# First batch of a fused linear-attention and ResMLP kernel: k^T v kept raw and times g in one operand, W_tok and W_ch1 loaded in pieces by GpSimd's queue, and the instruction order read from a table

## The chip, the core and the metric

The kernel runs on one core of one Trainium2 chip. The metric is the device time of one execution in microseconds (us). TensorE (PE) does the matmuls, VectorE (DVE), ScalarE (ACT) and GpSimd (POOL) the rest; SyncE (SP) and GpSimd issue the DMAs, each in the order of its own queue.

## The reference, cut to what matters

```python
# q, k, v: [8 batches, 8 heads, 576, 64];  x: [8, 576, 512]
kv  = einsum('bhsd,bhse->bhde', k, v)
out = einsum('bhsd,bhde->bhse', q, kv)
rms = sqrt(mean(out * out, axis=-1, keepdims=True) + 1e-06)
x   = (out / rms * g_norm)            # heads side by side: [8, 576, 512]
a1  = alpha1 * x + beta1
u   = x + lam * einsum('ts,bsd->btd', w_tok, a1)       # token mixing, 576 x 576
a2  = alpha2 * u + beta2
y   = u + lam * (maximum(a2 @ w_ch1, 0) @ w_ch2)       # 512 -> 2048 -> 512
```

## The kernel before, in words

Everything is recorded as operations (class Op) with their reads and writes, and then put in order. Batch after batch the stages are: kv (k^T v for pairs of heads, two heads to a matmul, only the diagonal blocks kept, in `kvc`), norm (q times kv, squares, sums, square root, reciprocal, and the scaling to x and to r, the operand of the token mixing), tok (token mixing with the transposed W_tok in `wt`, then the addition to x), a2 (alpha2, beta2 and the transposition of u), ch1 (64 matmuls of 512 columns against W_ch1, ReLU on ScalarE) and ch2 (64 matmuls against W_ch2; finish multiplies by lam, adds and stores). A main tile of 512 tokens goes by batch; the last 64 tokens of two batches go together (the tail: ch1_tail, and column group c = 4 of ch2).

**Batch 0 is done in halves** (j = 0, 1: four heads each), so that the first channel matmuls can begin early. load_half (L616) brings q, k and v in pairs of heads of 288 KB through SP's queue. qt_early (L693) interleaves two pairs of q (L698, GpSimd) and transposes them on PE in fp32 (L703). kv_first (L719) multiplies k by v (L725) and copies the result to `kvc` (L736 DVE, L739 ACT). norm_half (L854) makes q.kv in matmuls of 128 columns (L864), and norm_ops (L793) follows: Square (L807 ACT), sum (L810 DVE), Sqrt (L813 ACT), reciprocal (L816 DVE), x (L828 DVE), r = x times e1 (L831, GpSimd or DVE), x times g (L833, GpSimd). e1 is the row alpha1 x lam x 8 g, spread over the partitions by a matmul (L678). wt_group (L1077) transposes W_tok, loaded in fp32 by one DMA on SP's queue (L629) and one for the last 64 rows (L631), by fp32 transposes on PE (L1081, L1084), and ACT copies them (L1087). wsums (L1097) makes column sums of it (L1103, L1105) for the beta1 term; these go to rows of `wt` (L1110 ACT, L1113 DVE), and every token mixing reads them with its fifth slice. tok_half (L924) is the token mixing of a half (L929, addition L937 on DVE), a2_pair (L965) the transposition of u (L968 PE, L972 ACT).

Batch 1 has its q pairs loaded and transposed as in batch 0 (L703, L713), its k and v by GpSimd's queue (L1186, L1190); kv(1) is L749 and L755, norm(1) L843. From batch 1 on, a2_dma (L976) makes a2 by two GpSimd passes (L986, L989) and a transposing DMA (L993). W_ch1 and W_ch2 are cast to bf16 by their DMAs, which only GpSimd's queue issues (L1163, L1169); W_ch1 comes as one quarter, one quarter and one half.

**The order.** `schedule` (L135) plans the program when it is built: due times, a list of hand-set shifts (L1283) and gates (L1298, extra dependencies), and costs in us decide which operation each engine takes next. PE takes "main" matmuls (ch1, ch2) in their order and fits "fill" matmuls (all others) between or weaves a float32r or fp32 one with a bf16 one. Until the first main matmul, idle time of PE and the gaps of fp32 matmuls are filled with matmuls of 128 columns on a constant tile `fil` (L597, here called fillers; `fil` is set by the memset L596). Every engine then executes its own list in order; an instruction that waits holds up all behind it on its engine.

Of the kernel before, what the change touches and what calls it, by code (L numbers as in the profile page):

```python
# [7 lines left out]
F32 = mybir.dt.float32  # L8
# [7 lines left out]
NH = 8  # L16
# [7 lines left out]

class Op:


    __slots__ = ("bias", "q", "kind", "cost", "lat", "fns", "pri", "idx", "deps", "raw", "alloc",
                 "tiles", "start", "end", "pos", "waits", "inc", "clock", "slot", "nbytes",
                 "val", "margin", "tag", "narrow", "urgent", "ns")  # L30

    def __init__(self, q, kind, cost, lat, fns, pri, idx):
        self.q, self.kind, self.cost, self.lat = q, kind, cost, lat
        self.fns, self.pri, self.idx = fns, pri, idx
        self.deps, self.raw = set(), set()
        self.alloc, self.tiles = [], []
        self.start = self.end = self.pos = None
        self.waits, self.inc, self.clock = [], False, None
        self.slot = self.nbytes = self.val = self.ns = None
        self.margin = 0.0  # L40
        self.tag, self.narrow, self.urgent = "", False, False
# [12 lines left out]
class Prog:  # L54
    ENGINES = ("PE", "ACT", "DVE", "POOL")

    def __init__(self, nc, stack):
# [7 lines left out]
        self.main, self.fill = [], []  # L65
        self.bias = 0.0
        self.reach = 24
        self.warm, self.began, self.early, self.lead = 6.0, False, 45.0, 100.0
        self.t0, self.pace, self.last, self.shift = 31.0, 1.28, None, {}
        self.gate = {}  # L70
# [4 lines left out]
    def _add(self, o, r, w, after):  # L75
# [10 lines left out]
        for key in w:  # L86
# [5 lines left out]
            for y in self.readers.get(key, ()):  # L92
                if y is not o:
                    o.deps.add(y)
                    if not isinstance(key, Bank) and key[0] == "sm":
                        o.raw.add(y)
# [11 lines left out]
    def op(self, q, cost, fn, r=(), w=(), pri=0.0, lat=0.15, after=()):  # L108
        o = Op(q, "c", cost, lat, [fn], self.bias + pri, len(self.ops))
        o.bias = self.bias  # L110
        return self._add(o, r, w, after)

    def dma(self, q, slot, nbytes, fn, r=(), w=(), pri=0.0, after=(), issue=0.55):
        o = Op(q, "d", issue, 0.0, [fn], self.bias + pri, len(self.ops))
        o.slot = slot
        o.nbytes, o.ns = nbytes if isinstance(nbytes, tuple) else (nbytes, 20.0)
        o.bias = self.bias
        return self._add(o, r, w, after)

    def mm(self, stream, cols, fns, r=(), w=(), slow=False, after=(), margin=0.3,  # L120
           urgent=False):

        n = len(fns)
        per = cols * MM_NS + 0.0025
        each = slow if isinstance(slow, float) else {"r": 0.213}.get(slow, 0.109)
        o = Op("PE", "w" if slow and each is not slow else "m",
               n * (max(per, each) if slow else max(per, 0.056)),
               0.24, fns, self.bias, len(self.ops))
        o.bias = self.bias
        o.margin, o.narrow, o.urgent = 0.0 if urgent else margin, cols < 512, urgent  # L130
        (self.main if stream == "main" else self.fill).append(o)
        return self._add(o, r, w, after)


    def schedule(self):  # L135
        for i, j in self.gate.items():
            self.ops[i].deps.add(self.ops[j])
        due, t = {}, self.t0
        for o in self.main:
            due[o] = t  # L140
            t += o.cost * self.pace
        after = {}
        for o in self.ops:
            for y in o.deps:
                after.setdefault(y, []).append(o)
        order, left = [], {o: len(after.get(o, ())) for o in self.ops}
        stack = [o for o in self.ops if not left[o]]
        while stack:
            o = stack.pop()
            order.append(o)  # L150
            for y in o.deps:
                left[y] -= 1
                if not left[y]:
                    stack.append(y)
        for o in order:
            d = due.get(o, 1e6)
            for y in after.get(o, ()):
                if y in due:
                    d = min(d, due[y] - o.cost - o.lat - (2.5 if o.kind == "d" else 0.0))
            if d < 1e6:  # L160
                due[o] = d
        for o in self.ops:
            if o.kind == "d":
                o.pri += self.shift.get(o.idx, 0.0)
            elif o in due and o.pri - o.bias > -900:
                o.pri = due[o] + self.shift.get(o.idx, 0.0)
            elif o.pri - o.bias > -900:
                o.pri = 1e4 + o.pri
        self.fill.sort(key=lambda o: o.pri)
        queues = {e: [] for e in ("ACT", "DVE", "POOL", "SP")}  # L170
        for o in self.ops:
            if o.q != "PE":
                queues[o.q].append(o)
        for q in queues.values():
            q.sort(key=lambda o: (o.pri, o.idx))
        main, fill = list(self.main), list(self.fill)
        self.main0 = set(self.main)
        free = {e: 0.7 for e in list(queues) + ["PE"]}
        owner = [None] * 8
        rings = {e: deque() for e in ("SP", "POOL", "ACT")}  # L180
        t, left = 0.0, len(self.ops)
        events = {0.7}
        self.sequence = []
        self.idle = []
        last_fill = False
        INF = 1e9

        def ready_at(o):
            m = 0.0
            for y in o.deps:  # L190
                if y.end is None:
                    return INF
                m = max(m, y.end - y.lat if y.q == o.q == "PE" else y.end)
            return m

        def bank_at(b):
# [1137 lines left out]
```

## Time and profile before

| what | us |
|---|---|
| three runs | 356.01, 356.05, 357.27 |
| median of the runs | 356.05 |
| profiled execution, first to last instruction (its span) | 354.8 |
| so outside the span, against the median | 1.25 |
| PE busy in the span | 341.3 |
| DVE, POOL, ACT busy | 189.8, 161.4, 149.0 |

Busy time of PE counts a matmul from its start to its modelled end, and matmuls overlap; so the rate is read from start to start, and a busy PE may be doing fillers. "Chain" below is the profile's chain of work that ended last, followed back from the last instruction: start, duration, what. In the table of stretches each engine has its busy time and, in brackets, its instructions, then the granted clock of PE, the share of the DMA engines and GB/s.

### The profile page before, as it was taken

The page shows a single profiled execution, that of the slowest core. Times are in us where ns is not written, and L with a number is a line of the kernel's source. Part 1 is how long each engine was busy: PE and PEld are TensorE (multiplying, and loading weights), DVE is VectorE, ACT ScalarE, POOL GpSimd, SP SyncE. Part 2 cuts the span into 40 slices and gives each one's busy share as a digit, 9 for nine tenths or more (in the row PEclk, how much of TensorE's full clock was granted, in tenths as well). Part 3 has the DMA queues.
Part 4 walks back from the last instruction along what each step waited for, and adds up shares of the span by engine and source line. Part 5 has one row for each costly group of instructions (what it writes and reads, how often), then busy time and mean ns, then how long its engine had stood idle before and what let it go on. Part 6 is the DMA issues. An engine that isn't in the chain of part 4 may idle for free.

```text
span 354.8 us, 5512 instructions
## 1 busy us (share of the span) xinstructions
PE 341.3 (96%) x2208; PEld 198.4 (56%) x2241; DVE 189.8 (54%) x343; ACT 149.0 (42%) x291; POOL 161.4 (45%) x151
## 2 busy tenths in 40 slices
PE   4979999999999999999999999999999999999994
PEld 3858964454664664466556545564476444444644
DVE  3475778204685579636745676459444963210043
ACT  3335397004940386126823366136552273026400
POOL 2397410965308940985058612973192306930000
PEclk9989999999999999999999999999999999999999
DMA  7999899969598399138963995239922110330012
GB/s 241 267 336 161 139 251 230 144 110 198 120 262 134 90 232 213 31 93 195 247 61 76 221 173 124 46 116 258 175 33 89 59 31 15 75 105 0 2 69 79
DMA packets 107952, 48.76 MB, mean 137 GB/s; under 512 B 81997, under 2 KB 99925, under 8 KB 107928
## 3 DMA queue, kind: packets, MB, share of 16 engines
q1 hardware_dynamic: 82312, 27.71, 42.9%
q0 software_dynamic: 25616, 20.71, 34.0%
q8 instruction: 17, 0.28, 0.3%
q14 instruction: 7, 0.06, 0.1%
HBM read 38.82 MB, written 9.44 MB: 136 GB/s over the span
## 4 chain that ended last, share of the span: by engine, by line
PE 87%; DMA 5%; SPq 2%; POOL 2%; DVE 1%; issue 1%; ACT 0%; DVEq 0%; POOLq 0%
PE ps L1031 31%; PE ps L1002 31%; PE ps L914 8%; PE ps L1014 4%; PE ps L843 3%; DMA hh<-in_moe_w_tok_dram 2%; PE ps L749 2%; DMA w<-in_k_dram 2%; PE ps L597 1%; SPq L611 1%; PE ps L929 1%; POOL a1f L986 1%; PE ps L948 1%; PE ps L1081 1%; PE ps L1042 1%; DMA lam_bc<-in_moe_lam_dram 1%
## 5 line engine op out<-in xcount | busy, mean ns | idle before, releaser
L1031 PE MATMUL ps<-w,hh 128*128 128x512 bf16 x543 | 135.3, 383 | 0.7 <-issue 0.3
L1002 PE MATMUL ps<-a2m,w 128*128 128x512 bf16 x501 | 117.8, 381 | 1.0 <-DVE tmp L1058 0.4
L997 ACT ACTIVATE hh<-ps 128x512 bf16<-128x512 f32 x144 | 84.8, 597 | 64.3 <-PE ps L1002 54.9
L1031 PEld LDWEIGHTS ps<-w,hh 128*128 128x128 bf16 x560 | 52.9, 97 | 58.8 <-issue 1.6
L1002 PEld LDWEIGHTS ps<-a2m,w 128*128 128x128 bf16 x512 | 48.7, 98 | 56.5 <-DVE tmp L1058 1.3
L986 POOL TENSOR_TENSOR a1f<-xm,a_bc 128x512 f32<-128x512 f32 x28 | 35.5, 1273 | 68.6 <-DVE xm L921 68.3
L1058 DVE TENSOR_TENSOR tmp<-ps,lam_bc 128x512 f32<-128x512 f32 (+2 forms) x38 | 25.1, 661 | 69.8 <-PE ps L1031 56.5
L1063 POOL TENSOR_TENSOR xm<-xm,tmp 128x512 f32<-128x512 f32 x28 | 35.4, 1269 | 34.7 <-DVE tmp L1058 34.7
L810 DVE TENSOR_REDUCE small<-sq 128x8 f32<-128x512 f32 (+2 forms) x41 | 27.2, 666 | 25.2 <-ACT sq L807 25.0
L989 POOL TENSOR_TENSOR a2b<-a1f,b_bc 128x512 bf16<-128x512 f32 x32 | 40.3, 1273 | 0.7
L843 PE MATMUL ps<-kvc,qt 128*128 128x128 f32 x140 | 40.1, 395 | 0.0
L921 DVE TENSOR_TENSOR xm<-ps,xm 128x512 f32<-128x512 f32 x28 | 19.3, 690 | 29.8 <-PE ps L914 28.5
L749 PE MATMUL ps<-vr,kr 128*128 128x128 f32 x112 | 32.3, 395 | 0.0
L807 ACT ACTIVATE sq<-ps 128x512 f32<-128x512 f32 (+2 forms) x41 | 23.9, 584 | 19.3 <-PE ps L843 18.5
L1199 ACT ACTIVATE qt<-qp 128x576 fp32r<-128x576 f32 x24 | 15.9, 682 | 32.3 <-DVE qp L1196 32.3
L843 PEld LDWEIGHTS ps<-kvc,qt 128*128 128x128 f32 x140 | 27.4, 199 | 2.0
L914 PE MATMUL ps<-rm,wt 128*128 128x512 bf16 x109 | 28.3, 379 | 0.2
L597 PE MATMUL ps<-fil 128*128 128x128 bf16 x109 | 20.0, 245 | 4.5 <-DVE fil L596 4.5
L819 DVE TENSOR_TENSOR ps<-ps,small 128x512 f32<-128x512 f32 (+1 forms) x35 | 23.5, 690 | 0.5
L766 ACT ACTIVATE kvo<-ps 64x256 f32<-64x256 f32 x14 | 5.3, 378 | 43.0 <-PE ps L755 42.8
L749 PEld LDWEIGHTS ps<-vr,kr 128*128 128x128 f32 x112 | 22.3, 201 | 0.9
L1196 DVE STREAM_TRANSPOSE qp<-qs 128x576 f32<-128x576 f32 x24 | 17.3, 755 | 5.6 <-DMA qs<-in_q_dram 3.4
(109 smaller groups left out, 324.0 us busy)
## 6 DMA issues: line engine op xcount, KB each, us to landing
out_dram<-xm SPq DMA_DIRECT2D x32, 256.0 KB, 2.3
kr<-in_k_dram POOLq DMA_DIRECT2D x7, 1024.0 KB, 9.0
vr<-in_v_dram POOLq DMA_DIRECT2D x7, 1024.0 KB, 11.4
qs<-in_q_dram SPq DMA_DIRECT2D x24, 288.0 KB, 11.1
w<-in_moe_w_ch_dram POOLq DMA_DIRECT2D x3, 1024.0 KB, 10.2
xm<-in_q_dram SPq DMA_DIRECT2D x8, 288.0 KB, 4.4
w<-in_k_dram SPq DMA_DIRECT2D x4, 288.0 KB, 5.6
qs<-in_v_dram SPq DMA_DIRECT2D x4, 288.0 KB, 5.9
```

Source lines behind the costliest of these rows:

```text
L749: P.mm("fill", 128, [lambda e, t=t, c=c, h=h, o=128 * (h % 4): e.matmul(t.ap()[:, o:o + 128], kr4[:, h, c:c + 2, :].rearrange("p c d -> p ...
L807: P.op("ACT", act(n), lambda e: e.activation(sq[rs, s3, 0:nst, :].rearrange("p h e -> p (h e)"), ps(), ACT.Square), r=[t], w=[("sq", s3)])
L810: P.op("DVE", dve(n), lambda e: e.tensor_reduce(out=st, in_=sq[rs, s3, 0:nst, :], axis=AX.X, op=ALU.add), r=[("sq", s3)], w=[("sm", s4)])
L843: P.mm("fill", 128, [lambda e, p=p: e.matmul(dst(p), qt[:, p, cs], kvc[:, i, p, :], start=(p == 0), stop=(p == 3)) for p in range(4)], r=[ ...
L914: P.mm("fill", 512, [lambda e, sc=sc: e.matmul(t.ap(), wt[:, sc if sc < 4 else tw(b), 128 * c:128 * c + 128], rsrc(b, sc, al), start=(sc = ...
L986: P.op("POOL", pool(512), lambda e: e.tensor_tensor(out=a1f[:, s], in0=x, in1=a2_bc[:], op=ALU.mult), r=ks + ["a2"], w=[("a1f", s)])
L989: P.op("POOL", pool(512), lambda e: e.tensor_tensor(out=a2b[:, c], in0=a1f[:, s], in1=b2_bc[:], op=ALU.add), r=[("a1f", s), "b2"], w=[("a2 ...
L997: P.op("ACT", act(512), lambda e: e.activation(dst, t.ap(), ACT.Relu), r=[t], w=keys, pri=-1000)
L1002: P.mm("main", 512, [lambda e, dj=dj: e.matmul(t.ap(), w1[:, dj, 128 * fj:128 * fj + 128], a2m[:, b % 3, dj, :], start=(dj == 0), stop=(dj ...
L1031: P.mm("main", 512, [lambda e, fj=fj, t=t, c=c: e.matmul(t.ap(), (ht[:, fj, 128 * c:128 * c + 128] if c < 4 else hl[:, fj, :]), w2[:, fj, ...
L1058: P.op("DVE", dve(z - a), lambda e: e.tensor_tensor(out=tmp[:, s, a:z], in0=t.ap()[:, 0:z - a], in1=lam_bc[:, a:z], op=ALU.mult), r=[t, "l ...
L1063: lambda e: e.tensor_tensor(out=x, in0=x, in1=tmp[:, s, a:z], op=ALU.add),
```

## The change

The scheduler is gone; `replay` takes the order of all 1439 operations with their PSUM banks from a table (ORDER), with fillers written as ~n and woven matmuls as a+b, and a new list of gates (GATES). Besides:

- kv_first writes k^T v twice: raw (ACT, `kvc` slot 0) and times 8g (DVE, slot 1). norm_half multiplies q by both in one float32r matmul of 256 columns; the squares are taken from the raw half, x = (q.kv.g) times the reciprocal, and r = x times `la` (alpha1 x lam) is one GpSimd pass. The GpSimd pass x times g of batch 0 is gone. g comes by a broadcast DMA; e1 for the later batches is la x g, one GpSimd pass.
- W_tok is cast to bf16 by three DMAs on GpSimd's queue (behind a gate: the last copy of the first half's k^T v). Its transposes are bf16 matmuls against a bf16 identity, `idb`; the copies alternate between ACT and DVE.
- tok_half is cut in two matmul groups, the slices 0 to 3 and the slice 4, so that only the second waits for the column sums. a2_pair alternates ACT and DVE.
- W_ch1 and W_ch2 come in quarters. In batch 1, r of the four main column groups is a GpSimd pass, the addition of tok goes to PSUM and a1f is made from there by DVE, with a copy to x by ACT.
- In the odd batches ch2 takes column group 4 before 3, so that the last tile, which is cut in three, is a main one of 128 rows with one store each.

```diff
-        P.schedule()
+        P.replay(ORDER, GATES)
...
+ORDER = """
+33 3 7 4 30 14 0 27 ~35 13 6 5 32 12 28 15 204 10 1 29 9 2 31 203 35 8 17 11 34 41 42 16 59:1 18
...
+GATES = {12: 4, 16: 15, 18: 6, 22: 58, 26: 203, 37: 35, 38: 21, 39: 44, 40: 1, 122: 142, 184: 74,
...
+    def replay(self, order, gates):
+        for i, j in gates.items():
             self.ops[i].deps.add(self.ops[j])
+        for word in order.split():
+            if word[0] == "~":
+                self.sequence.append((self.idler(int(word[1:])),))
+                continue
+            unit = []
+            for part in word.split("+"):
...
+                at, *banks = part.split(":")
+                o = self.ops[int(at)]
...
+        for c in (0, 2):
+            P.dma("POOL", "wl%d" % c, dcost(256, 105), lambda e, c=c: e.dma_start(
+                wl[:, c:c + 2, :], moe_w_tok[128 * c:128 * c + 256, :].rearrange(
+                    "(c p) s -> p c s", p=128)), w=[("wl", c), ("wl", c + 1)], issue=0.9)
+        P.dma("POOL", "wlt", dcost(64, 190), lambda e: e.dma_start(
+            wlt, moe_w_tok[512:576, :]), w=["wlt"], issue=0.8)
...
+                    raw, dst = (kvc[rs, i, 2 * j + s, 64 * m:64 * m + 64] for i in range(2))
+                    P.op("ACT", act(64), lambda e, raw=raw, src=src: e.activation(
+                        raw, src(), ACT.Identity), r=[t], w=[("kv%d" % m, 0, 2 * j + s)])
+                    P.op("DVE", dve(64), lambda e, dst=dst, src=src, rs=rs: e.tensor_tensor(
+                        out=dst, in0=src(), in1=g_bc[rs, :], op=ALU.mult), r=[t, "g"],
...
             P.mm("fill", 128, [lambda e, c=c, cs=cs, s=s: e.matmul(
-                dst(c, s), qt[:, 2 * j + s, cs], kvc[:, 0, 2 * j + s, :],
+                dst(c, s), qt[:, 2 * j + s, cs], kvc[:, :, 2 * j + s, :],
...
+            P.op("POOL", pool(w), lambda e: e.tensor_tensor(
+                out=r, in0=x, in1=la_bc[rs, None, fs].to_broadcast([rs.stop - rs.start, n, 256]),
...
-            for c in range(2 * ch, 2 * ch + 2):
+            for scs in (range(4), (4,)):
...
-        load_w1(0, 1, q2)
-        load_w1(1, 1, q3, 1)
+        load_w1(0, 1)
         for p in range(4):
-            load_pair(1, "q", q, q1s, p, k3)
-        load_w1(2, 2, v3, 2)
+            load_pair(1, "q", q, q1s, p)
+        for i in range(1, 4):
+            load_w1(i, 1)
...
-            cs = range(5 if b % 2 else 4)
+            cs = (0, 1, 2, 4, 3) if b % 2 else (0, 1, 2, 3)
```

Read out in words, the table gives these orders up to the second batch's channel matmuls. **PE:** 35 fillers; the spreading of la; 9 transposes of q (half 0); k^T v of half 0 with 5 and 10 fillers behind its two pairs; 9 transposes of q (half 1); q.kv of column groups 4, 2 and 3 of half 0; k^T v of half 1; q.kv of groups 0 and 1 of half 0; 14 fillers; q.kv of groups 2 and 3 of half 1; the 25 W_tok transposes, with 9, 5, 7 and 3 fillers and the rest of q.kv of half 1 among them; column sums and token mixing of half 0 (slices 0 to 3, then 4); 14 of the 18 q transposes of batch 1; then, in turns, two a2 transpositions of half 0, the token mixing of half 1, and ch1 on the first two a2 pieces; the other two a2 transpositions; the rest of ch1. kv(1) stands late in ch1 (three of its five groups woven with ch1, two alone), norm(1) in ch2 (two of five groups alone), then tok(1), 12 ch2 matmuls, kv(2) with all five groups alone, and ch1 of batch 1. **GpSimd:** the W_tok loads; r of group 4; a q copy; r of groups 2 and 3; the four W_ch1 quarters (gate: x of groups 2 and 3); r of groups 0 and 1; then the three other q copies among r of half 1 (groups 2 and 3, groups 0 and 1, group 4); k and v of batch 1; the four W_ch2 quarters. **DVE:** the memset of `fil` is third.

More of the change, by code (lines that the diff above doesn't have):

```diff
@@ L121, in mm @@
            urgent=False):
[L123 to L131, printed above, removed]
+        o = Op("PE", "m", 0.0, 0.0, fns, self.bias, len(self.ops))
```

599 lines of the change are left out of this document (202 added, 397 removed), and 88 rows, old and new, of tables (GATES, ORDER, cs).

## The prediction, as it was put on record

> **What bounds the kernel now.** First the page (span and PE's row), then the table of stretches (granted clock third from the end).
>
> ```profile
> span 354.8 us, 5512 instructions
> PE   4979999999999999999999999999999999999994
> ...
> 4.50:22.00 17.50, 16.89 (x224) 13.72 (x224) 7.13 (x17) 7.06 (x19) 7.65 (x10) 1.00 0.94 290
> 22.00:24.00 2.00, 0.05 (x1) 0.05 (x2) 1.38 (x5) 0.97 (x3) 1.31 (x3) 1.00 1.26 361
> 24.00:28.00 4.00, 4.00 (x29) 3.27 (x30) 1.80 (x2) 0.80 (x2) 3.22 (x4) 0.57 1.78 361
> 28.00:44.40 16.40, 16.30 (x171) 14.69 (x172) 11.30 (x22) 6.65 (x15) 9.35 (x10) 1.00 0.99 134
> 44.40:81.80 37.40, 36.82 (x198) 19.80 (x202) 18.60 (x32) 15.06 (x30) 16.64 (x16) 1.00 1.00 183
> 81.80:350.40 268.60, 267.29 (x1591) 146.91 (x1618) 145.92 (x256) 116.95 (x222) 121.87 (x105) 1.00 0.71 117
> ```
>
> From 44.4 us to 350.4 PE lacks 1.9 of 306 us: it is the bound there, at full clock, and its work is fixed. Before 44.4 its full digits deceive: the groups of instructions of the head, and who PE waited for, say why.
>
> ```profile
> L597 PE MATMUL ps<-fil 128*128 128x128 bf16 x109 | 20.0, 245 | 4.5 <-DVE fil L596 4.5
> ...
> PE ps L597 <- DVE fil L596: 4.5, 1, 4.5
> PE ps L1081 <- DMA hh<-in_moe_w_tok_dram: 2.0, 1, 2.0
> ```
>
> 109 of its head's matmuls are fillers. So the head's length is a chain of other things, with PE along for the ride. The chain of waits names it (start, duration).
>
> ```profile
> 15.58 8.33 DMA hh<-in_moe_w_tok_dram
> 23.95 0.33 PE ps L1081
> ...
> 31.73 0.81 PE ps L1103 x3
> ...
> 44.37 0.38 PE ps L1002
> ...
> 44.75 0.87 PE ps L968 x8
> ...
> 81.78 10.57 PE ps L1002 x48
> ...
> 333.02 10.74 PE ps L1031 x49
> ```
>
> W_tok lands at 23.9, its transposes and copies last until the column sums at 31.7, and the first channel matmul is at 44.4. Two marks follow from it: the first channel matmul (44.4) and the first of batch 1 (81.8). Whatever moves the second moves the end one for one.
>
> The time is taken from this execution, of 354.8 us; 1.25 us lie between it and the median of 356.05 shown, and I leave them as they are.
>
> **The change, part by part: the head.** Durations used:
>
> ```profile
> 3.67 0.66 POOL L698 COPY hh<-xm 128x576 f32<-128x576 f32 x1 [2.21 <-DMA xm<-in_q_dram]
> ...
> 8.82 2.02 PE L725 MATMUL ps<-qs,w 64*64 64x64 f32 x36 [0.28 <-DMA qs<-in_v_dram]
> 10.93 1.26 PE L725 MATMUL ps<-qs,w 64*64 64x64 f32 x36
> ...
> 24.17 0.41 PE L1081 MATMUL ps<-ident,hh 128*128 128x128 f32 x1
> ...
> 24.48 0.42 PE L1081 MATMUL ps<-ident,hh 128*128 128x128 f32 x1
> ...
> L807 ACT ACTIVATE sq<-ps 128x512 f32<-128x512 f32 x8 | 4.8, 596 | 1.3 <-PE ps L843 0.7 <-PE ps L864 0.6
> L810 DVE TENSOR_REDUCE small<-sq 128x8 f32<-128x512 f32 x8 | 5.4, 686 | 2.0 <-ACT sq L807 1.9
> L828 DVE TENSOR_TENSOR xm<-ps,small 128x512 f32<-128x512 f32 x4 | 2.7, 687 | 0.1
> L831 POOL TENSOR_TENSOR rm<-xm,e_bc 128x512 bf16<-128x512 f32 x2 | 2.5, 1266 | 0.0
> L1163 POOL DMA_DIRECT2D w<-in_moe_w_ch_dram x3 | 2.4, 794 | 3.4 <-ACT small L813 3.4
> DMA to landing us min/median/max: 5.5/5.5/10.0
> ```
>
> Pairs of heads: the first is there at 3.67, the sixth at 8.82, so 1.03 us each; the twelfth, of half 1, at 3.67 + 11 x 1.03 = 15.0. The new order doesn't change this. The fillers start some 3 us sooner, since their memset is third; the first k^T v then takes 1.26 instead of 2.02. With v of the second pair in at 9.9, k^T v of half 0 ends at 11.3 and its last copy at 11.8. That copy now releases W_tok.
>
> W_tok on GpSimd's queue: the last row is W_ch1's three casting loads, of 512, 512 and 1024 KB. Doubling the size, issued right behind, made it 10.0 from 5.5; less the 2.6 us that one quarter lies in front, 1 MB takes 5.3 of transfer, 512 KB 2.6, and 2.9 is lead. Two pieces of 288 KB and one of 72 KB take 3.4 us: issued from 11.8, all in by about 18.5, or 19 beside the last pairs. So the landing moves from 23.9 to 19, and the 2.0 us stall with the half clock behind it (0.57 in the table) goes; late next is k of half 1.
>
> Half 1: k^T v from 15.3 to 16.6, copies to 18.1, q.kv to 18.9. Behind it, in PE's order, 25 transposes as bf16 matmuls. Before shows none; the bounds are a filler's slot and the fp32 one of 0.31 start to start, cold. I take 0.07, the filler's side, because a filler has their shape and type. With 24 fillers and q.kv of the last groups PE is through at 23, ACT and DVE have copied the five groups by 23.1 (0.6 to 0.7 each, alternately, beside the norm), column sums 23.6 to 24.6, token mixing of half 0 behind it; its slice 4 waits for ACT and DVE to write the sums' rows, 27.1. q.kv at 256 columns: 20 matmuls at between no more and twice the 0.15 of a lone one (rows below); I took 0.2, half of them on this path, so 0.5 less to 1 more.
>
> GpSimd is the second string. Its string starts with x of groups 2 and 3, at 17.2 (their q.kv at 13.9, then Square 0.6, sum 0.7, root 0.3, reciprocal 0.2 and x 0.7, and as much again behind group 4): r 1.27, four W_ch1 issues 3.2, r 1.27, then three q copies of 0.67 and one r of 1.27, 25.6 to 27; r of groups 0 and 1 of half 1 waits for its x at 28.1 (Square 0.6, sum 0.69, root, x 0.69, behind DVE's other work), so 29.4, and group 4 30.1. Four x times g passes of 1.35 less stood in this queue before. Token mixing of half 1 starts at 30.1, takes 1.1 twice with one transposition of u between (0.45, half the 0.87 above): **the first channel matmul at 33.0**, when ACT too has the two a2 pieces. The gain is 44.4 - 33.0 = 11.4.
>
> W_ch1's quarters are issued by 22.4 and land every 2.6 us, plus three q pairs of batch 1: the last at 34, wanted at 36. k and v of batch 1 land by 42 to 43 and are wanted at 43.5; W_ch2's first at 44 for 49. If these covers went, each us late would be a us of PE.
>
> **The change, part by part: what is left over.** kv(1) and norm(1)'s first group were done in the head; now they come behind the first channel matmul. What a float32r matmul costs there:
>
> ```profile
> 120.91 0.41 PE L755 MATMUL ps<-vr,kr 128*128 128x128 f32 x1
> 121.20 0.41 PE L755 MATMUL ps<-vr,kr 128*128 128x128 f32 x1
> ...
> 123.80 0.75 PE L843 MATMUL ps<-kvc,qt 128*128 128x128 f32 x4
> 124.39 1.04 PE L1002 MATMUL ps<-a2m,w 128*128 128x512 bf16 x4
> ```
>
> Woven, it and a bf16 one take 0.29 together; 49 bf16 ones alone take 10.74, 0.22 each: so 0.07. Alone, four take 0.59, 0.15 each. Then kv(1) is 12 x 0.07 + 8 x 0.15 = 2.1; norm(1)'s first group 0.6, its second, now alone, 0.3 more; four q transposes left, 0.44; kv(2), now all alone, 20 x 0.08 = 1.5 more. Sum 4.9.
>
> Then two waits are added. tok(1) waits for batch 1's norm, which began before the channel matmuls and now begins at 52.9.
>
> ```profile
> 44.28 0.60 ACT L807 ACTIVATE sq<-ps 128x512 f32<-128x512 f32 x1 [0.51 <-PE ps L843]
> ...
> 60.01 0.68 DVE L825 TENSOR_TENSOR xm<-ps,g_bc 128x512 f32<-128x512 f32 x1
> ```
>
> There it took 60.7 - 44.3 = 16.4 us. Four r of 0.69 are now GpSimd's, and x of the last group isn't waited for: 13. PE comes from 33.0 through 64 ch1 matmuls (14.1), kv(1), two a2 and four q transpositions (3.4) and 8 ch2 matmuls (1.7) to norm(1) at 52.2; two lone groups (1.2), three woven with 24 ch2 matmuls (6.1) and 20 more (4.3) bring it to tok(1) at 63.9, the norm ends at 65 to 66. I take 1.0, the middle of nothing and 2. Queued behind are 12 ch2 matmuls that could have filled it. The second wait is for a2 of batch 1 (add and a1f on DVE, 1.27 on GpSimd, transposing DMA) against 12 matmuls and kv(2): 0.6. The steady state has as many lone groups as before.
>
> The Trainium skill, "TensorE: Matmul & The Clock Gate", section "What's actually happening", says that PE's clock is halved after an idle window of some 3.4 us and restored by as long a busy one. By that rule neither wait costs clock, and the sum stays; by the row of 24 to 28 us an idle time of 2.0 was enough, at 0.43 x 4 = 1.7 us, which would be added. The trace thus disagrees with the length, and I keep 1.7 as an upper end.
>
> At the end a last tile of one store a part in place of two saves an issue, 0.4 as an estimate from the DMA issues in SP's queue (0.3 to 0.5), nothing to 0.6.
>
> **Sum:** -11.4 + 4.9 + 1.0 + 0.6 - 0.4 = -5.3; 354.8 - 5.3 = 349.5 of span, **350.7 us**. Open bounds: the first channel matmul 3 us either way, the waits -1.6 to +2.7.
>
> **The rivals.**
>
> *Head and waits better.* DVE, with fewer head passes, reaches x of groups 0 and 1 three us sooner, and GpSimd hides it; tok(1) doesn't wait. 346.7. For it: DVE is busy only 11.3 of the 16.4 us after 28, so its part of the string has slack. Against: the GpSimd string has four issues in its middle.
>
> *W_tok late.* GpSimd's load starts only behind k^T v, beside the last pairs. If it takes the 8.3 us of the old load, and the pieces queue, 21.5 to 22 instead of 19: 2.7 later, and PE idles from 19 and goes to half clock, 1.1 to 1.7. 354.9. For it: the half clock at 24 to 28 after such a stall. Against: W_ch1's 5.5 us. The Trainium skill, "SBUF — State Buffer", section on the ports, warns that DVE in some modes stops GpSimd from writing descriptors, which would make loads from GpSimd's queue late; by that rule this rival gains, but W_ch1's issues took 0.75 to 0.83 us with DVE busy 11.3 of 16.4 us, so I leave it its chance.
>
> *The change takes less waste than it seems* (it doesn't do what it says): kv(1) and q.kv filled waiting PE in the head, and are now paid in full, while the first channel matmul only comes to 39, because slice 4 and GpSimd's string lag each other. 356.
>
> *Slower: batch 1's chain is uncovered.* Place: tok(1) to the first channel matmul of batch 1. From batch 1's first Square to that matmul it was 81.8 - 44.3 = 37.5 us, hidden under ch1 and ch2; I give it 24 (52.9 to about 76.5). Only the last 12 ch2 matmuls, the tail of tok and kv(2) stand there as cover. At 28.9 the gain is gone, above 30.7 the kernel is over 0.5% slower; at 33 it is 360. For it: lam's load came late in the same chain,
>
> ```profile
> 77.35 3.54 DMA lam_bc<-in_moe_lam_dram
> ```
>
> and finish stands ahead of a2 in GpSimd's queue. Against: lam now has a gate that opens at 52.
>
> **How the numbers follow.** Forecast 0.55 (own range 347.5 to 354), better 0.14, W_tok late 0.12, less waste 0.09, slower 0.10. Half a per cent, 1.78 us, is what a measurement can tell from no change: faster is below 354.27. Forecast and better give 0.69, and a third of the late case falls below too, 0.73; the same has 0.17; slower 0.10. The range leaves out the slow case and the best half of the better one: 346.5 to 356.5.
>
> **What would show it.** W_tok's last piece landed by 19 and no PE idle over 1 us before 33; the clock at 1.00 from 24 to 28; the first channel matmul at 30 to 36; batch 1's at 74 to 79; PE waits for DVE at tok(1) of up to 2 us. Wrong: a first channel matmul after 38, or a PE wait of over 4 us between 50 and 85.

## The result, and the profile after

The changed kernel took 352.87 us (median of 21 runs, 350.92 to 358.19), the kernel before 355.90 beside it (21 runs, 353.63 to 358.09): a ratio of 0.992, 95% interval 0.990 to 0.994. A second series gave 353.72 (12 runs) against 355.74, 0.995 (0.992 to 0.998). So it is faster by 0.5 to 0.8%, 2 to 3 us, where 5.3 were forecast. The execution profiled in the first series was a disturbed one, so all rows of "after" are from the profile of the second series, of the same kernel: 352.5 us of span, 354.26 of time.

The page, then the table of stretches, cut at the two marks of the prediction (first channel matmul, first of batch 1); granted clock third from the end:

```profile
span 352.5 us, 5507 instructions
PE   8979999988999999999999999999999999999996
```

```profile
4.50:22.00 17.50, 16.90 (x230) 13.59 (x229) 5.36 (x20) 8.78 (x24) 9.74 (x13) 1.00 0.83 244
22.00:24.00 2.00, 0.50 (x7) 0.33 (x7) 1.17 (x2) 0.00 (x0) 2.00 (x3) 1.00 0.75 168
24.00:28.00 4.00, 3.46 (x37) 2.67 (x38) 2.55 (x5) 2.59 (x8) 2.33 (x4) 1.00 1.16 230
28.00:36.05 8.05, 8.05 (x72) 6.75 (x70) 6.92 (x14) 3.55 (x8) 6.53 (x8) 1.00 1.20 205
36.05:78.02 41.97, 40.67 (x232) 22.95 (x231) 21.97 (x40) 19.32 (x37) 21.04 (x22) 1.00 1.22 208
78.02:349.48 271.46, 269.75 (x1618) 147.10 (x1618) 144.72 (x252) 117.04 (x222) 119.19 (x103) 1.00 0.69 114
```

The first mark is at 36.05 (forecast 33.0, before 44.37), the second at 78.02 (76.9; 81.78). PE again stands still for most of 22 to 24 us. The last stretch is the surprise: from the second mark to PE's last matmul 271.46 us, where before took 350.34 - 81.78 = 268.56 for the same matmuls. Whom PE waited for (total, times, longest):

```profile
PE ps L969 <- DMA hh<-in_moe_w_tok_dram: 2.0, 1, 2.0
PE ps L888 <- DMA a2m<-a2b: 1.0, 1, 1.0
PE ps L900 <- DMA a2l<-a2b: 1.0, 1, 1.0
PE ps L695 <- ACT qt L1092: 0.6, 1, 0.6
PE ps L583 <- DMA w<-in_k_dram: 0.4, 1, 0.4
PE ps L778 <- DVE rtl L679: 0.3, 1, 0.3
```

L447 is now the filler, L561 the fp32 transpose, L583 k^T v, L969 the W_tok transpose, L721 q.kv of batch 0, L778 tok(1), L888 ch1, L900 ch1_tail, L917 and L928 ch2. The stall on W_tok, which was to go, is there with the same 2.0 us. Three waits of 2.6 us in all are at or behind the second mark: a2, the a2 of the tail, the q copy. The head in order of time:

```profile
7.24 2.18 PE L561 MATMUL ps<-ident,hh 128*128 128x128 f32 x9
9.78 2.19 PE L583 MATMUL ps<-qs,w 64*64 64x64 f32 x36 [0.36 <-DMA w<-in_k_dram]
...
12.55 1.44 PE L583 MATMUL ps<-qs,w 64*64 64x64 f32 x36
...
14.49 1.15 PE L561 MATMUL ps<-ident,tmp 128*128 128x128 f32 x9
...
24.54 1.40 PE L969 MATMUL ps<-idb,hh 128*128 128x128 bf16 x14 [2.04 <-DMA hh<-in_moe_w_tok_dram]
```

The reading lies in the pairs: the same nine transposes take 2.18 us at 7.24 and 1.15 at 14.49. The first k^T v takes 2.19 for a forecast 1.26. PE ran at half speed until 12.96 us: there the trace's own list of clock changes begins, with the change to full, and the column counts all that lies before it as 1.00. Two equal groups of a timeline show what that column doesn't.

At the end, PE's last matmul to the end of the span took 354.8 - 350.34 = 4.46 us before and 352.5 - 349.48 = 3.02 after.

### The profile page after: what moved, and what is told of

It is laid out like the page before. It is cut to its first block, busy times and chain, and to the rows that moved or that the text cites. A ratio compares the mean times of both kernels' runs of the same rounds, so it can differ in the third digit from the quotient of the medians.

```text
span 356.4 us, 5507 instructions
## 1 busy us (share of the span) xinstructions
PE 344.4 (97%) x2218; PEld 198.1 (56%) x2218; DVE 186.3 (52%) x344; ACT 153.3 (43%) x300; POOL 162.5 (46%) x154
## 4 chain that ended last, share of the span: by engine, by line
PE 83%; DMA 6%; DVE 4%; POOL 3%; ACT 1%; SPq 1%; issue 1%; DVEq 0%
PE ps L917 31%; PE ps L888 29%; PE ps L778 8%; PE ps L900 4%; PE ps L695 3%; DMA hh<-in_moe_w_tok_dram 2%; DMA w<-in_k_dram 2%; PE ps L605 2%; POOL a2b L875 2%; DMA qs<-in_q_dram 2%; PE ps L801 1%; PE ps L583 1%; POOL xm L950 1%; PE ps L823 1%; PE ps L928 1%; DVE ps L674 1%
## 5 line engine op out<-in xcount | busy, mean ns | idle before, releaser
L917 PE MATMUL ps<-w,hh 128*128 128x512 bf16 x560 | 136.6, 382 | 0.0
L888 PE MATMUL ps<-a2m,w 128*128 128x512 bf16 x512 | 119.1, 381 | 1.0 <-DMA a2m<-a2b 1.0
L888 PEld LDWEIGHTS ps<-a2m,w 128*128 128x128 bf16 x512 | 47.0, 98 | 53.5 <-DMA a2m<-a2b 1.1
L917 PEld LDWEIGHTS ps<-w,hh 128*128 128x128 bf16 x560 | 48.1, 98 | 51.4 <-issue 1.6
L868 POOL TENSOR_TENSOR a1f<-xm,a_bc 128x512 f32<-128x512 f32 x24 | 30.4, 1274 | 73.1 <-DVE xm L788 72.9
L695 PE MATMUL ps<-kvc,qt 128*128 128x128 f32 x140 | 45.0, 393 | 0.6 <-ACT qt L1092 0.5
L666 DVE TENSOR_REDUCE small<-sq 128x8 f32<-128x512 f32 (+1 forms) x35 | 23.5, 677 | 23.7 <-ACT sq L663 23.6
L663 ACT ACTIVATE sq<-ps 128x512 f32<-128x512 f32 (+1 forms) x35 | 20.6, 594 | 20.2 <-PE ps L695 20.2
L778 PE MATMUL ps<-rm,wt 128*128 128x512 bf16 x112 | 28.9, 379 | 0.3 <-DVE rtl L679 0.3
L788 DVE TENSOR_TENSOR xm<-ps,xm 128x512 f32<-128x512 f32 x24 | 16.5, 690 | 21.4 <-PE ps L778 21.4
L605 PEld LDWEIGHTS ps<-vr,kr 128*128 128x128 f32 x112 | 20.1, 195 | 5.0
L624 DVE TENSOR_TENSOR kvc<-ps,kvo 64x256 fp32r<-64x256 f32 x14 | 5.9, 421 | 26.4 <-ACT kvo L622 26.3
```

The costliest lines, as they stand in the source:

```text
L605: P.mm("fill", 128, [lambda e, t=t, c=c, h=h, o=128 * (h % 4): e.matmul(t.ap()[:, o:o + 128], kr4[:, h, c:c + 2, :].rearrange("p c d -> p ...
L666: P.op("DVE", dve(n), lambda e: e.tensor_reduce(out=st, in_=sq[rs, s3, 0:nst, :], axis=AX.X, op=ALU.add), r=[("sq", s3)], w=[("sm", s4)])
L695: P.mm("fill", 128, [lambda e, p=p: e.matmul(dst(p), qt[:, p, cs], kvc[:, i, p, :], start=(p == 0), stop=(p == 3)) for p in range(4)], r=[ ...
L778: P.mm("fill", 512, [lambda e, sc=sc: e.matmul(t.ap(), wt[:, sc if sc < 4 else tw(b), 128 * c:128 * c + 128], rsrc(b, sc, al), start=(sc = ...
L868: P.op("POOL", pool(512), lambda e: e.tensor_tensor(out=a1f[:, s], in0=x, in1=a2_bc[:], op=ALU.mult), r=ks + ["a2"], w=[("a1f", s)])
L888: P.mm("main", 512, [lambda e, dj=dj: e.matmul(t.ap(), w1[:, dj, 128 * fj:128 * fj + 128], a2m[:, b % 3, dj, :], start=(dj == 0), stop=(dj ...
```

## The experiments

Two theories at first. **A**: the missing 2 to 3 us are lost in the head, where PE starts cold, waits for k and gets W_tok late. **B**: they are lost behind batch 1's first channel matmul. Later **C** joined: a wait costs clock besides its own length, but only in some executions. In the table of order, 49 is the first k^T v, 22 the first W_tok load, 234 to 237 the q loads of batch 2, 307 the transposing DMA of batch 1's last a2 piece, 376 to 380 kv(2), 358, 368 and 360 the last ch2 matmuls of batch 0, 473 the first ch1 of batch 1. Marks are of each kernel's one profile; times are medians, ratios against the kernel before in the same series.

| kernel | us (runs) | ratio, 95% | first ch1 | ch1 of batch 1 | from there to PE's last | span |
|---|---|---|---|---|---|---|
| after | 353.72 (12) | 0.995 (0.992 to 0.998) | 36.05 | 78.02 | 271.46 | 352.5 |
| b_fill | 354.16 (12) | 0.993 (0.989 to 0.997) | 34.12 | 76.08 | 270.08 | 349.2 |
| c_wtok | 352.56 (6) | 0.992 (0.989 to 0.995) | 35.37 | 78.19 | 270.89 | 352.0 |
| d_q2 | 356.27 (12) | 1.001 (0.998 to 1.005) | 34.01 | 78.66 | 271.66 | 353.3 |
| e_k0 | 352.89 (12) | 0.993 (0.990 to 0.997) | 34.26 | 76.44 | 270.90 | 350.4 |
| f_head | 350.83 (6) | 0.988 (0.983 to 0.993) | 32.22 | 73.96 | 271.31 | 348.3 |
| g_late | 358.88 (6) | 1.011 (1.006 to 1.017) | 37.56 | 79.31 | 275.01 | 357.3 |
| h_weave | 353.07 (12) | 0.993 (0.990 to 0.996) | 35.83 | 77.56 | 270.87 | 351.4 |
| i_fillc | 350.51 (6) | 0.985 (0.982 to 0.989) | 32.07 | 73.80 | 270.95 | 348.5 |
| j_both | 350.69 (6) | 0.986 (0.982 to 0.989) | 32.34 | 74.08 | 270.18 | 347.9 |
| l_nofill | 351.12 (6) | 0.986 (0.982 to 0.989) | 33.20 | 74.93 | 271.05 | 349.0 |

**a_same**, the changed kernel again, for the profile above.

> The changed kernel as it is, for a second profile and as the yardstick of the runs beside it: about 352.9 us. Theory A (the missing 2.3 us of the forecast are a cold head): where PE's clock is full from about 8 us on, the first channel matmul comes at 33 to 36 us instead of the 40.5 of the first profile, and what lies behind the first channel matmul of batch 1 is as long as before, 268.6 us to the last matmul's start of 350.4. Theory B (they are lost later): that stretch is again near 271 us, whatever the head does, with PE waits of 0.5 to 1 us between 82 and 96 us.

The profile has both theories' signs at once: 3.05 us late at the first mark, 2.9 lost behind the second.

**b_fill**: 24 more fillers ahead of the first k^T v.

```diff
-44 49:5:6 25
+44 ~24 49:5:6 25
```

> 24 fillers more on PE in front of the first k^T v, in the time in which it waits for k (2.3 us in the first profile); nothing else changes. Theory A: the clock stays full, the first two k^T v take 1.3 us instead of 2.2 each, and the time falls by 1.5 to 3 us against a_same. Theory B: the head is a chain of DMA landings that the clock hardly moves; less than 0.5 us either way. A price of the fillers themselves, where PE hadn't waited: at most 24 x 0.056 = 1.3 us more.

In its profile no wait for k or W_tok is left, the first k^T v takes 1.26 us, the first mark is at 34.12, and the span of 349.2 is 0.3 from the forecast's 349.5. W_tok's issue in after, then in b_fill with the transposes that need it:

```profile
15.33 1.62 POOL L483 DMA_DIRECT2D hh<-in_moe_w_tok_dram  x2 [2.61 <-DVE kvc L595]
```

```profile
15.56 1.62 POOL L483 DMA_DIRECT2D hh<-in_moe_w_tok_dram  x2 [3.21 <-DVE kvc L595]
22.58 1.43 PE L969 MATMUL ps<-idb,hh 128*128 128x128 bf16 x14
```

So the load isn't issued sooner than in after; it is only faster, its second piece in 7.0 us after the first issue where after took 9.2. And only four of b_fill's times lie near its profile (350.2 to 351.2); five others are at 353.9 to 354.8, three above 356, and its median is no better: what one profile shows is one of several ways in which an execution goes.

**c_wtok**: W_tok's load without its gate.

```diff
-GATES = {... 18: 6, 22: 58, 26: 203 ...}
+GATES = {... 18: 6, 26: 203 ...}
```

> The gate that holds W_tok's first load until the last copy of half 0's k^T v is taken away; GpSimd issues it behind its second q copy, about 3 us sooner. Theory A (W_tok is late on GpSimd's queue): the 2.1 us wait of the W_tok transposes goes, with the half clock behind it; 2 to 3.5 us less than a_same. Rival: the three loads then share the DMA engines with k and v of half 1, which come later by as much, 1 us less to 1 us more.

The wait for W_tok is gone and the times lie closer (351.68 to 353.82). But here PE waited 2.4 us for k, the two pairs of k^T v took 2.18 and 2.19, and the first mark is at 35.37. W_tok's load didn't do that: it is issued at 13.09, when both pairs of k are in (10.16), and d_q2, which has the gate, waits 2.7 us for k. In both PE's clock was full early (5.58 and 4.34), so that PE was through with the q transposes about 2 us sooner than in after and waited for a k that lands at 9.7 to 10.2.

**d_q2**: the three later q loads of batch 2 without gates, ahead of a2's transposing DMAs on SP's queue.

```diff
-236 372 275 ... 379 237 235 380 ... 383 234 381
+236 237 235 234 372 275 ... 379 380 ... 383 381
...
-GATES = {... 234: 306, 235: 369, 236: 245, 237: 370 ...}
+GATES = {... 236: 245 ...}
```

> The gates on three of the four q loads of batch 2 are taken away and the loads stand in SP's queue right behind the first (ahead of the transposing DMAs of batch 1 and of two stores). Theory B: the chain q load, DVE transposition, ACT copy, norm of batch 2 comes sooner, the PE waits of 0.5 us for ACT and 0.6 us for a2 of the tail at 91 to 95 us shrink, and the time falls by 0.5 to 1.5 us against a_same. Theory A: these waits are noise beside the head, under 0.3 us.

Slower than after. The waits for the q copy and the tail's a2 go, as B says, but the loads hold the queue (SP's instructions: start, duration):

```profile
58.12 11.65 SPq L1071 DMA_DIRECT2D qs<-in_q_dram  x4
69.82 2.27 SPq L954 DMA_DIRECT2D out_dram<-xm  x1
72.13 5.26 SPq L879 DMA_TRANSPOSE a2m<-a2b  x4
```

The first transposing DMA starts 72.13 - 64.44 = 7.7 us behind tok(1), 71.51 - 66.48 = 5.0 in after. PE waits 3.65 us for a2, and the first 40 channel matmuls behind the wait take 10.86 us in place of 8.81.

**e_k0**: the first pair of k swaps places with the second in SP's queue. (The text on record says "ahead of the second pair of q"; that pair, of the same half, stays ahead. What k passes is the second pair of k and the first of v.)

```diff
-10 1 29 9 2 31 203 35 8 17
+1 29 8 9 10 2 31 203 35 17
```

> One edit to the kernel after: SP issues the first pair of k as its third load, ahead of the second pair of q. Theory A (the head stays cold: PE waits for k, then multiplies k^T v at half clock): the wait for k of 0.4 to 2.4 us goes, the first k^T v takes 1.26 us in place of 2.18, and the first channel matmul comes at 34 to 35 us in place of 36.05; the time falls by 1 to 2 us from 353.7. Theory B (what is missing is lost after batch 1's first channel matmul): the head may move, but no more than 0.5 us reaches the end, since q of the second pair is now late by the transfer that passed it, about 1 us.

The wait for k goes, yet k^T v takes 2.19 and then 1.88: PE was cold without having waited. The first mark comes at 34.26, mainly since W_tok isn't waited for in this profile, though it is issued at 15.49.

**f_head**: b_fill, c_wtok and e_k0 together.

> Three edits at once to the kernel after: k third in SP's queue, 24 more fillers ahead of the first k^T v, and W_tok's load without its gate. Theory A: no wait of PE for k or W_tok is left, the granted clock is 1.00 from 5 us on, the first channel matmul comes at 33 to 34.5 us in every execution, and the times lose their upper group (354 to 356) and lie at 350 to 352. Theory B: the first channel matmul comes as early, but the time stays at 353 to 354, as the waits behind batch 1's channel mixing stay. A third possibility, that loads compete: with W_tok in front, k or v of the first pairs lands over 1 us later, PE waits 2 us or more and goes cold, and the first channel matmul stays at 35 to 36.

Theory A's numbers hold in the main: 350.83, five of six runs at 349.6 to 351.6 (one at 353.1), and the first mark at 32.22. Its head, against the rows of after:

```profile
6.57 1.20 PE L561 MATMUL ps<-ident,hh 128*128 128x128 f32 x9
7.61 1.50 PE L447 MATMUL ps<-fil 128*128 128x128 bf16 x24
9.04 1.26 PE L583 MATMUL ps<-qs,w 64*64 64x64 f32 x36
```

But something new is behind the second mark. The table of stretches of f_head, PE's wait for a2 in its first row:

```profile
73.00:74.00 1.00, 0.04 (x2) 0.04 (x2) 0.52 (x2) 0.76 (x2) 1.00 (x2) 1.00 0.52 135
74.00:75.00 1.00, 1.00 (x3) 0.37 (x4) 0.46 (x2) 0.00 (x0) 0.83 (x1) 0.55 1.00 227
...
76.00:77.00 1.00, 1.00 (x4) 0.43 (x3) 0.00 (x0) 0.38 (x1) 0.90 (x1) 0.50 1.52 150
77.00:78.00 1.00, 1.00 (x5) 0.35 (x3) 0.00 (x0) 0.51 (x1) 0.00 (x0) 0.75 1.66 141
```

and of after, the same wait:

```profile
77.00:78.00 1.00, 0.04 (x1) 0.00 (x0) 0.48 (x2) 0.76 (x2) 1.00 (x2) 1.00 0.63 141
78.00:79.00 1.00, 0.98 (x5) 0.51 (x6) 0.45 (x2) 0.00 (x0) 0.89 (x1) 1.00 0.92 219
```

Waits of 0.96 and 0.98 us at the same place: in one execution the clock halves for 3.4 us behind it (0.45 x 2 + 1 + 1 + 0.25 x 2), in the other not at all. This is theory C. It has little behind it: with after, seven profiles have a wait of 0.96 to 1.83 us at this place and no half clock (b_fill, c_wtok, e_k0, g_late, h_weave and l_nofill are the others), and f_head's five other executions, 349.6 to 353.1 us, are all listed with a granted clock of 1.000, where one spell of 3.4 us makes 0.995.

**g_late**: the transposing DMA of the tail's a2 ahead of the last q load.

```diff
-379 237 235 380 ... 383 234 381 ... 466 307 485:4
+379 380 ... 383 381 ... 466 237 235 307 234 485:4
```

> One edit to the kernel after: on SP's queue the transposing DMA of batch 1's last a2 piece goes ahead of the last of the three q loads of batch 2 and behind the other two. Theory B: the wait of 1.0 us for that a2 piece, which PE has 10 us behind batch 1's first channel matmul, goes; from that matmul to the last stretch of ch2 it takes 266.6 to 267.0 us in place of 267.92; the time falls by about 1. The wait for the q copy on ACT (0.6) may grow by up to 0.5. Theory A: the wait moves to that q copy in full, and nothing is gained.

A miss of my own making: by this edit the q loads came to stand behind batch 0's next store too, which waits for GpSimd. After, then g_late:

```profile
77.41 4.85 SPq L1071 DMA_DIRECT2D qs<-in_q_dram  x3
82.31 1.84 SPq L954 DMA_DIRECT2D out_dram<-xm  x1
84.19 1.22 SPq L879 DMA_TRANSPOSE a2l<-a2b  x1
```

```profile
78.08 4.53 SPq L954 DMA_DIRECT2D out_dram<-xm  x2
82.65 1.97 SPq L1071 DMA_DIRECT2D qs<-in_q_dram  x2
84.67 2.41 SPq L879 DMA_TRANSPOSE a2l<-a2b  x1
```

The q loads start 5.2 us later, and PE's wait for the q copy is 3.5 us, for the tail's a2 1.7: from the second mark to PE's last matmul 3.5 us more than after. It doesn't test its question (j_both does), but it gives a price: q loads 5.2 us later cost 3.5 us there.

**h_weave**: three of kv(2)'s groups woven with the 12 ch2 matmuls ahead of them.

```diff
-299 358 292 ... 283 368 293 304 360 294 ... 376:4 370 ... 377 378:2 306
+299 376:4+358 292 ... 283 377+368 293 304 378:2+360 294 ... 370 ... 306
```

> One edit to the kernel after: three of kv(2)'s five groups (12 float32r matmuls) are woven with the 12 ch2 matmuls ahead of them, in place of standing alone behind them. If PE's own work decides when batch 1's channel mixing starts (as the forecast's term of 1.5 us for kv(2) alone says), tok(1) to the first channel matmul of batch 1 takes 10.7 us in place of 11.54 and the time falls by 0.9. If the chain to a2 decides (addition, a1f, GpSimd's pass, transposing DMA), it stays at 11.5, and PE's wait for a2 grows from 1.0 to 1.8 us.

tok(1) to the first channel matmul of batch 1 takes 77.56 - 66.04 = 11.52, in after 78.02 - 66.48 = 11.54, and the wait for a2 grows:

```profile
PE ps L888 <- DMA a2m<-a2b: 1.3, 1, 1.3
```

So the chain to a2 decides there, and kv(2) alone, for which I charged 1.5 us, is paid by nobody: less work of PE is more waiting. The wait grew by 0.3, not by the 0.8 expected. In after 16 matmuls of kv(2) alone take 76.44 - 74.51 = 1.93 us, 0.12 each and not the 0.15 that q.kv takes alone, so weaving saves less than I counted.

**i_fillc**: f_head, and 16 fillers between kv(2) and the channel matmuls.

```diff
-381 473:6 384
+381 ~16:6 473:6 384
...
```

> The three edits of f_head, and 16 fillers (0.9 us at full clock) between kv(2) and the first channel matmul of batch 1, where PE waited 0.96 us for a2. Theory C (a wait of 1 us can halve the clock for the 3.4 us behind it, in some executions and not in others, as the grid of the clock's stretches falls): the fillers take the wait's place, the channel matmuls of batch 1 start as before (11.5 us behind tok(1)), their first 40 take 8.7 to 8.8 us in place of 10.5, from the first of them to the end of PE's work it is 269.5 in place of 271.3, and the times lie at 348 to 350 us, closer together than those of f_head. Theory D (the half clock there had another cause than that wait): it comes again in the profile, or the times stay at 350.8.

The first 40 channel matmuls take 8.81 us again and no stretch is at half clock; but seven profiles without these fillers show none there either. The times, 349.65 to 352.22 with a median of 350.51, lie above the 348 to 350 of theory C; beside f_head's 350.83, of another series, they can't be told apart, which is theory D's second sign. All six have a granted clock of 0.998 or more, so half-clock spells don't spread them. Of the 10.49 - 8.81 = 1.7 us, waits of 0.4 (tail's a2) and 0.7 (q copy) take 1.1, which in f_head had passed under the slow matmuls: 270.95 us to PE's last matmul in place of 271.31. Its profile also has 0.7 us more behind that matmul (the two stores ahead took SP 1.90 us in place of 1.12), and j_both's has 0.6; neither edit explains it.

**j_both**: i_fillc, and 307 right behind 234.

```diff
-383 234 381 ... 466 307 485:4
+383 234 307 381 ... 466 485:4
```

> As i_fillc, and the transposing DMA of batch 1's last a2 piece stands on SP's queue right behind the third q load of batch 2, ahead of the store that it followed. Theory B (the waits behind batch 1's first channel matmul are worth about 1 us): no wait for that a2 piece in the profile, the wait for the q copy as it was (0.4 to 0.9), and up to 0.5 us less than i_fillc in the times. Rival: the waits are covered in i_fillc already, or move to the q copy, and the two kernels agree within 0.5 us.

In the profile the wait for the tail's a2 is gone, that for the q copy 0.5; 270.18 us in place of 270.95. The times, 350.69 beside 350.51 in the same series, don't show it: there the rival is right.

**k_tail**: the kernel before, with the change's last tile alone.

```diff
-            cs = range(5 if b % 2 else 4)
+            cs = (0, 1, 2, 4, 3) if b == 7 else range(5 if b % 2 else 4)
...
```

> The kernel before with one part of the change alone: in the last batch ch2 takes the column group of 64 + 64 tokens ahead of the last main tile, so that the tile cut in three is stored by three DMAs and not six. Forecast's term: 0.4 us less (0 to 0.6). By the two profiles, which have 4.46 us from PE's last matmul to the end before and 3.02 after: 1.4 us less, with three issues of 0.6 us gone from the end of SP's queue. Nothing else moves: 268.6 us from batch 1's first channel matmul to PE's last.

354.35 us against 356.32, ratio 0.994 (0.991 to 0.997). SP's end, before and k_tail:

```profile
349.48 3.68 SPq L1071 DMA_DIRECT2D out_dram<-xt  x6
```

```profile
348.90 1.13 SPq L1071 DMA_DIRECT2D out_dram<-xt  x2
350.11 1.85 SPq L1066 DMA_DIRECT2D out_dram<-xm  x3
```

Its last six issues ended at 353.16, 2.2 us behind DVE's last addition (350.97); now the queue follows DVE to 351.96, 0.4 behind its last addition at 351.60. PE's last matmul to the end: 353.6 - 350.95 = 2.65 us, 4.46 before. This edit alone is worth about 2 us by the times, 1.8 by the profile; the whole change brought 2 to 3.

**l_nofill**: f_head without the 38 fillers behind k^T v of half 1.

> The three edits of f_head, less the 38 fillers that stand among the W_tok transposes and q.kv of half 1 (2.1 us of PE at full clock). If PE's own order sets the first channel matmul, it comes 2 us sooner, at 30.2 in place of 32.22, and the time falls by as much. If the GpSimd string (r, W_ch1's issues, q copies, r) sets it, as the forecast says, it stays at 32 and PE shows waits of some 2 us in the sum; and if these waits halve the clock, it comes at 33 to 34 and the times spread.

The start of the column sums (L995), f_head and l_nofill:

```profile
23.81 0.81 PE L995 MATMUL ps<-wt,pick 128*128 128x512 bf16 x3
```

```profile
23.82 1.49 PE L995 MATMUL ps<-wt,pick 128*128 128x512 bf16 x3 [0.24 <-DVE small L746]
```

With 2.1 us less of PE's work they start at the same time: the strings on the other engines set the head, as the forecast says. But PE, now with gaps of 0.9 and 0.6 us, is at half clock from 22.5 to 26, and the first mark comes at 33.20. In this profile the fillers buy clock, not time; the times (351.12, and 350.83 for f_head in another series) can't be told apart.

## Why the prediction was right and where it was wrong

| mark | forecast | after | f_head |
|---|---|---|---|
| W_tok waited for until | 19 | 24.5 | not waited for |
| first channel matmul | 33.0 | 36.05 | 32.22 |
| from it to tok(1), with its wait | 31.9 | 30.43 | 30.21 |
| from there to ch1 of batch 1 | 12.0 | 11.54 | 11.53 |
| from there to PE's last | 268.56 | 271.46 | 271.31 |
| from there to the end | 4.06 | 3.02 | 3.03 |
| span | 349.5 | 352.5 | 348.3 |

**Right:** the sign, the engine that bounds, the second mark (78.02, in 74 to 79) and the order of size of what is left over: 4.9, 1.0 and 0.6 us more between the two marks were forecast, 6.5 in all, and 41.97 - 37.41 = 4.6 measured. The wait at tok(1) is 0.32, at the low end of nothing to 2, and the clock is 1.00 from 24 to 28. The string of column sums (23.6 forecast) is at 23.8 in f_head, and 33.0 for the first mark is bettered there by 0.8; but f_head is not the change. In the change's own profile the first mark, 36.05, lies just outside its bounds of 30 to 36, and PE idles 2.0 us before 33, where no idle time over 1 was to be.

**Failed, first step:** W_tok in by 19, and no stall of PE. It was issued at 15.3, not 11.8, and its second piece landed at 24.5, 9.2 us later and not 7. The issue is late for three reasons. "The new order doesn't change this" fails: v of the second pair lands at 11.2, not 9.9. "The first k^T v then takes 1.26 instead of 2.02" fails: PE was still cold at 9.8, k was 0.4 late, and it took 2.19. And the copies, now raw and times g in turns, end 1.2 us behind k^T v, not 0.5. But the late issue alone stalls nobody: b_fill, d_q2 and e_k0 issue at 15.0 to 15.6, the second piece is in 6.0 to 7.0 us later, and PE doesn't wait. Their first marks are at 34.0 to 34.3, so some 1.9 of the 3.05 are the stall, and 1.1 are there without it. What made the load take 9.2 in after the traces don't show. My rival "W_tok late" named the consequence (PE idle until the load is in, 2.7 us later) and a load of 8.3 us. f_head, without the gate and with PE warm, shows that the plan's head can be reached, by other edits than the change.

**Failed, second step:** "Whatever moves the second mark moves the end one for one". After the second mark the same matmuls take 2.9 us more. It is lost early: from the mark to the first ch1_tail matmul of batch 3, 174.46 - 78.02 = 96.44 us, before 175.69 - 81.78 = 93.91, so 2.5; from there to that of batch 7, 153.93 against 153.55. The rows:

```profile
87.79 1.51 PE L900 MATMUL ps<-a2l,w 128*128 128x128 bf16 x24 [0.96 <-DMA a2l<-a2b]
...
91.02 0.33 PE L695 MATMUL ps<-kvc,qt 128*128 128x128 f32 x1 [0.63 <-ACT qt L1092]
91.19 0.23 PE L900 MATMUL ps<-a2l,w 128*128 128x128 bf16 x1
91.23 0.30 PE L695 MATMUL ps<-kvc,qt 128*128 128x128 f32 x1
```

The two waits make 1.6 by the profile, but 1.9 from start to start, as the modelled end of a matmul lies behind the slot it takes. The 40 ch1 matmuls ahead of the first wait need 87.79 - 78.02 = 9.77 us with it, and 82.72 - 74.08 = 8.64 in j_both, where there is none. The four narrow ones ahead of the second take 91.02 - 90.00 = 1.02 in place of 4 x 0.06:

```profile
90.00 0.39 PE L900 MATMUL ps<-a2l,w 128*128 128x128 bf16 x4
```

```profile
74.08 8.81 PE L881 MATMUL ps<-a2m,w 128*128 128x512 bf16 x39
82.72 1.50 PE L893 MATMUL ps<-a2l,w 128*128 128x128 bf16 x24
```

(L881 and L893 are ch1 and ch1_tail in j_both; one record of 40 is missing.) The four float32r matmuls here are woven with the narrow ones of ch1_tail, 0.2 us a pair, of which the narrow one costs 0.06 (24 in 1.35): they are paid at 0.14 each, as if alone, which my count of lone groups didn't see, though that is only 4 x 0.07 = 0.3. Of the 2.5 us some 0.3 stay unexplained. That the waits are real costs is shown by j_both's profile, where one is gone and the stretch is 1.3 us shorter than in after; d_q2 shows that q in time is paid for by a2, both being on one queue.

**Mis-sized:** the tail, -0.4 (0 to 0.6), is -1.4 by the marks, and k_tail alone gives 1.8. I priced one issue saved, of 0.4; three of 0.6 are, and all three stood on the path, since SP's queue was 2.2 us behind DVE. Kv(2) alone with the wait for a2, 1.5 + 0.6, is not a sum: h_weave shows that the one is the cover of the other. And the time outside the span is not 1.25: in nearly every run for which both are on record it is 1.8, so 349.5 of span would have been 351.3.

So in the profile of after the head is 3.05 late, the middle 1.9 better, the last stretch 2.9 worse, the tail 1.0 better: 3.0 together, 352.5 for 349.5. That the time still lies in the range is in part luck: the middle and the tail, mis-sized to the good, gave back half of the 5.9 that the two failed steps cost. And this profile is a slower execution than most: the median of the first series, 352.87, means a span of about 351.1. What the sum held fixed was the pace of the loads, PE's clock at the start, and the next batch's queue behind the second mark.

**Open:** what groups the times. Half-clock spells go with them in the kernel before: in k_tail, which is before but for its last tile, the executions at a granted clock of 0.999 or 1.000 took 350.8 and 351.3 us, those at 0.994 or 0.995 353.2 to 354.1, those at 0.990 354.7 to 356.0. In the changed kernel and its variants they don't: b_fill's two groups both hold executions at 1.000. A cold start, which that column leaves out, and a slow W_tok load remain; no profile of one kernel in two groups shows which.

When PE becomes warm seems to hang on where the grid of the clock's spells falls. The first change to full clock is at 4.34 to 5.87 us in seven profiles (d_q2, j_both, l_nofill, g_late, c_wtok, f_head, i_fillc) and at 10.73 to 13.65 in four (b_fill, after, h_weave, e_k0), with the same 35 fillers from 1.4 to 5.2 us. A stretch of 3.41 us that ends at the change of the seven begins at 0.93 to 2.46 and lies in these fillers but for 0.6 us at most. Counted back from the change of the four in steps of 3.41, one begins at 2.72 to 3.90 and runs 0.9 us or more past them. No run with a longer row of fillers tests that.

## What to carry to other kernels

A load that waits behind a copy passes on everything that the copy's matmuls suffer; if it is to come early, issue it early, and leave room for one that takes 9 us where another execution takes 6. When a stage is pulled ahead, look at what shared its queue and its slack: the next batch's loads and transposing DMAs had both been hidden, and the gain of 3.8 us at the second mark shrank to 0.9 before it reached the end of PE's work. And look at the last issues of a queue: three DMAs fewer at the end were worth about 2 us, most of what the whole change brought.

## What the runs showed of the hardware

The half clock comes in spells of 3.4 us or twice that, at multiples of that length from each other. In d_q2, the rows in which the two spells begin and end:

```profile
11.00:12.00 1.00, 1.00 (x17) 0.81 (x17) 0.00 (x0) 0.18 (x1) 0.00 (x0) 0.58 1.05 412
...
14.00:15.00 1.00, 1.00 (x13) 1.00 (x11) 0.70 (x4) 0.47 (x4) 0.00 (x0) 0.71 0.11 32
...
76.00:77.00 1.00, 0.00 (x0) 0.00 (x0) 0.47 (x2) 0.00 (x0) 0.83 (x1) 0.51 0.65 131
...
82.00:83.00 1.00, 1.00 (x4) 0.40 (x3) 0.00 (x0) 0.60 (x1) 0.17 (x1) 0.58 0.50 183
```

With half speed inside a spell, 0.58 over a microsecond means 0.84 of it: the first spell lasts from 11.16 to 14.58, the second from 76.02 to 82.84, so 3.42 and 6.82, and they begin 64.86 us apart, 19 times 3.41. In the execution of f_head one follows a wait of 0.96 us; behind the same wait in after, and behind waits of up to 1.83 us there in six other profiles, there is none. The Trainium skill, "TensorE: Matmul & The Clock Gate", section "What's actually happening", says that activity is judged in free-running windows of 3413 ns, so that it varies from run to run where a change of clock falls. The spells agree with that length and with such a grid. Its idle time of a window of some 3.4 us before the clock is halved doesn't agree: the spell of the kernel before follows a wait of 2.0 us (after has such a wait without a spell), that of f_head one of 0.96.

The granted clock of a profile doesn't show the cold start: it reads 1.00 from 4.5 to 22 us in after, while the nine fp32 transposes take 2.18 us at 7.24 and 1.15 at 14.49. The list behind it begins with the first change to full, at 12.96.

A q.kv matmul of 256 columns in float32r takes 0.15 us start to start, the same as one of 128 columns alone (four in 0.59 in the prediction's rows), the lower of the two bounds that the prediction gave it (k^T v of 128 columns alone takes 0.12). In f_head six of 256 columns fill the 0.88 us to the next k^T v:

```profile
13.53 0.96 PE L721 MATMUL ps<-kvc,qt 128*128 128x256 f32 x6
14.41 2.59 PE L583 MATMUL ps<-qs,w 64*64 64x64 f32 x72
```
